# Dividing the score matmuls of the full-attention layers from 64 rows by 128 columns into 64 rows by 32 columns

## The chip, the cores and the metric

The kernel runs on one core of one Trainium2 chip. The metric is the device time of one execution in microseconds (us). Before the change the median of three runs is 2757.61 us (2755.26 to 2764.16).

The engines are named as the profile names them: PE is TensorE's matmul, PEld its weight load, DVE is VectorE, ACT is ScalarE, POOL is GpSimd, SP is SyncE, which issues the DMAs.

## The reference

Four attention layers follow each other on one sequence of 2048 tokens with 512 features: windowed, full, windowed, full. Each is a residual block, with 32 heads of 16 dimensions.

```python
def _B_ref(x, wqkv, wo):                      # the full layer
    qkv = transpose((x @ wqkv).reshape(B, S, 3, H, Dh), 2, 0, 3, 1, 4)
    scores = einsum("bhqd,bhkd->bhqk", q, k) * Dh ** -0.5
    p = softmax(scores, axis=-1)
    o = einsum("bhqk,bhkd->bhqd", p, v)
    return transpose(o, 0, 2, 1, 3).reshape(B, S, D) @ wo
...
x = x + _A_ref(_layernorm(x), A_wqkv, A_wo)   # a window of 256 keys
x = x + _B_ref(_layernorm(x), B_wqkv, B_wo)   # all 2048 keys
x = x + _A_ref(_layernorm(x), A_wqkv, A_wo)
x = x + _B_ref(_layernorm(x), B_wqkv, B_wo)
```

## The kernel before, in words

**A step of a full layer.** `attn_full` (line 750) goes through four chunks of 512 queries, eight groups of four heads, and sixteen tiles of 128 keys: 4 x 8 x 16 = 512 steps in a layer, 1024 in the two full layers (l = 1 and l = 3). A step has these parts:

- Two calls of `exps` (line 706), one for each pair of heads. A head's queries and keys lie in 64 rows: four for each of 16 dimensions, with the high and low halves of float16 and a row for a shift. Two heads fill the 128 partitions. So `exps` issues two matmuls (line 714), one on rows 0 to 63 and one on rows 64 to 127, each with 128 keys as its stationary columns and 512 queries streaming. They write a score tile `ps` of 128 keys by 2 heads by 512 queries, which takes two PSUM banks, a bank for each head.
- One exponential for each `exps` (line 718) on ACT, over 128x1024 values, from `ps` into the SBUF tile `e`.
- Four float32 matmuls (line 758) that multiply `e` with the values: 17 columns (16 dimensions and a column of ones for the denominator) over 128 rows. Head h writes partitions 32h onwards, so that the four lie side by side in column groups of 32. A float32 matmul is two records in the trace, so a step has eight. They accumulate over the sixteen key tiles in `acc[0]`.
- Pieces of side work: the projections and output products of this and the next layer. `mms` (line 419) issues them in full layers as four matmuls of 128 rows by 32 columns (line 429), side by side, into `acc[1]`.

The score matmuls thus use the array as 64 rows by 128 columns, and everything else in a full layer uses it as 128 rows by 32 columns.

**Order.** The order on PE is written out by hand (`manual_schedule`). `attention` (line 955) issues the scores of a step, then the value matmuls of two steps earlier (`flush(2)`), then as much side work as `Side.share` (line 924) allows. `share` pays from a budget by a clock of its own that adds up expected costs (`spent`). The change leaves those costs as they are. The tiles of the other engines are ordered by the framework.

**Buffers.** There are three score tiles: two in the pool `ps_s` and the one called `PH["third"]`; there are six `e` tiles. A score matmul waits until ACT has read the tile three `exps` earlier. After sixteen steps DVE transposes `acc[0]` (line 686), and the first value matmul of the next group of heads waits for that.

**Windowed layers.** `attn_win` uses the same `exps`, there with pieces of 128 to 384 queries, and its projections are 128 rows by 128 columns (line 432).

Of the kernel before, what the change touches and what calls it, by code (L numbers as in the profile page):

```python
# [19 lines left out]
P = 128  # L20
# [9 lines left out]
R = 64  # L30
# [156 lines left out]
def fast_path(ctx, tc, flag, a_x, a_wqkv, a_wo, b_wqkv, b_wo, out):  # L187
# [3 lines left out]
    nc = tc.nc  # L191
# [16 lines left out]
    XC, XN, V, O, OT, KM, PH = {}, {}, {}, {}, {}, {}, {"free": 0.0}  # L208
# [4 lines left out]
    def spent(us):  # L213
        clock[0] += us
        return us
# [490 lines left out]
    def exps(name, kt, qt, pr, pieces):  # L706

        turn["s"] += 1
        ps = PH["third"] if PH["full"] and turn["s"] % 3 == 0 else ps_s.tile([P, 2, QC], F32, name=f"s{name}", tag="s")
        w0 = min(p[3] for p in pieces)  # L710
        w1 = max(p[3] + p[2] for p in pieces)
        for kc, qc, wd_, s0 in pieces:
            for h in range(2):
                nc.tensor.matmul(ps[:, h, s0:s0 + wd_], kt[R * h:R * h + R, pr, kc:kc + P],  # L714
                                 qt[R * h:R * h + R, pr, qc:qc + wd_], start=True, stop=True)
        spent(0.27)
        e = pp.tile([P, 2, QC], F32, name=f"e{name}", tag="e", bufs=EB)
        nc.scalar.activation(e[:, :, w0:w1], ps[:, :, w0:w1], AF.Exp, scale=SCALE)  # L718
        return e
# [30 lines left out]
    def attn_full(l, c, qd, kt, qt, a):  # L750
        for j in range(NT):
            es_ = []
            for pr in range(2):
                es_.append(exps(f"{l}_{c}_{qd}_{j}_{pr}", kt[j // 8], qt, pr, [(j % 8 * P, 0, QC, 0)]))

            def pv(j=j, es_=es_):
                for h in range(4):
                    nc.tensor.matmul(a[32 * h:32 * h + DH + 1, :], V[l, qd // 4, j // 8][:, j % 8, 4 * (qd % 4) + h, :],  # L758
                                     es_[h // 2][:, h % 2, :], start=(j == 0), stop=(j == NT - 1),
                                     skip_group_check=True)  # L760
            yield pv
# [5 lines left out]
    def attn_win(l, c, qd, kt, qt, a):  # L767
        first = True
        for u, tiles in enumerate(WTILES):
            tiles = [p for p in tiles if c or p[0] >= 0]  # L770
            es_ = []
            for pr in range(2):
                e = exps(f"{l}_{c}_{qd}_{u}_{pr}", kt, qt, pr,
                         [(WIN + j * P, q * P, nb * P, s * P) for j, q, nb, s in tiles])
                ev = e.rearrange("p h (m n) -> p h m n", n=P)
                edges = [(s + b, q + b - j == 2) for j, q, nb, s in tiles for b in range(nb) if q + b - j != 1]
                for b, far in edges:
                    v = ev[:, :, b, :]
                    with tc.high_priority(HEAD_START):
                        if far:  # L780
                            nc.gpsimd.affine_select(v, v, pattern=[[0, 2], [-1, P]], compare_op=ALU.is_gt,  # L781
                                                    fill=0.0, base=0, channel_multiplier=1)
                        else:
                            nc.gpsimd.affine_select(v, v, pattern=[[0, 2], [1, P]], compare_op=ALU.is_ge,  # L784
                                                    fill=0.0, base=0, channel_multiplier=-1)
                es_.append(e)

            def pv(u=u, tiles=tiles, es_=es_):
                for x, (j, q, nb, s) in enumerate(tiles):
                    for h in range(4):  # L790
                        nc.tensor.matmul(a[32 * h:32 * h + DH + 1, q * P:(q + nb) * P],  # L791
                                         V[l, (4 * c + j) // 4][:, j % 4, 4 * qd + h, :],
                                         es_[h // 2][:, h % 2, s * P:(s + nb) * P],
                                         start=(u == 0 and x == 0), stop=(u == 2 and x == len(tiles) - 1),
                                         skip_group_check=True)
            yield pv
# [398 lines left out]
```

## Time and profile before

| what | value |
|---|---|
| median of the runs | 2757.61 us |
| span of the profiled execution | 2759.8 us, 0.08% above the median |
| PE, ACT, DVE, POOL busy | 96%, 86%, 35%, 20% of the span |
| score matmuls, all layers (line 714) | 5504, of which 4096 have 512 queries and lie in the full layers |
| exponentials, all layers (line 718) | 2432 |
| value matmul records of the full layers (line 758) | 8192 |
| granted clock of PE in the full layers | 1.00 |

The results list no time of the profiled execution beside its span; the span is used as its own time. The full layers lie from about 507 to 1456 us and from 1792 to 2741 us of the span. Records of PE overlap, since each includes its way through the array: rates are read from starts, or from the length of a merged run of matmuls less one record. "a*b" in a matmul row is rows by columns of the stationary operand.

### The profile page before, as it was taken

To read this page: it belongs to the slowest core of one execution; us is meant where nothing else is said; L and a number is where in the kernel's file an instruction comes from. 1 tells how busy PE (TensorE), PEld (TensorE's weight loads), DVE (VectorE), ACT (ScalarE), POOL (GpSimd) and SP (SyncE) were. 2 spreads that over 40 slices of the span, in tenths; PEclk is the share of its full clock that TensorE was granted. 3 is DMA by queue.
4 is the path that set the end of the run, shared out by engine and by line. 5 is a ranking of instruction groups with operands and counts; after the bars stand their busy time and mean duration, and the time that the engine had idled before them with its cause. 6 is when DMAs were issued, how large, how long until landed. Compare 5 with 4: busy or idle time off the path is not lost.

```text
span 2759.8 us, 59658 instructions
## 1 busy us (share of the span) xinstructions
PE 2636.2 (96%) x24358; PEld 782.5 (28%) x24358; DVE 956.6 (35%) x2059; ACT 2377.0 (86%) x2687; POOL 564.5 (20%) x1129
## 2 busy tenths in 40 slices
PE   8989999999999999999998898999999999999997
PEld 4333344322222222222223333522222222222221
DVE  7678765112131113112215676512222222222122
ACT  3566664799999999999995677399999999999997
POOL 2477672000000000000004677100000000000000
PEclk9999999999999999999999999999999999999999
DMA  6877676322232123212325464613333343333321
GB/s 222 218 251 222 197 229 186 123 71 88 86 102 88 62 82 108 85 60 91 103 67 177 146 190 131 184 62 105 110 112 122 120 123 101 102 110 114 98 95 56
DMA packets 317501, 344.78 MB, mean 125 GB/s; under 512 B 113056, under 2 KB 233376, under 8 KB 311200
## 3 DMA queue, kind: packets, MB, share of 16 engines
q1 hardware_dynamic: 317216, 340.86, 40.4%
q8 instruction: 193, 3.16, 0.5%
q14 instruction: 92, 0.75, 0.1%
HBM read 228.07 MB, written 96.99 MB: 118 GB/s over the span
## 4 chain that ended last, share of the span: by engine, by line
PE 74%; ACT 9%; DVE 6%; issue 5%; POOL 3%; DMA 3%; SPq 0%; ACTq 0%; DVEq 0%; POOLq 0%
PE acc L758 30%; PE s L714 19%; PE acc L429 10%; PE b L432 9%; ACT e L718 8%; PE acc L791 3%; PE bs L432 2%; POOL e L781 1%; DVE ot L686 1%; POOL e L784 1%; POOL wr L344 1%; DVE sp L528 0%; POOL w L346 0%; PE acc L550 0%; DMA kt<-kw 0%
## 5 line engine op out<-in xcount | busy, mean ns | idle before, releaser
L718 ACT ACTIVATE e<-s 128x1024 f32<-128x1024 f32 (+2 forms) x2432 | 2243.5, 1116 | 96.8 <-PE s L714 90.2
L758 PE MATMUL acc<-e,vt 128*17 128x512 f32 x8192 | 1078.0, 598 | 5.3 <-DVE ot L686 4.1
L714 PE MATMUL s<-qt,kt 64*128 64x512 f16 (+3 forms) x5504 | 780.5, 355 | 64.7 <-ACT e L718 41.8
L714 PEld LDWEIGHTS <-kt 64*128 64x128 f16 x5504 | 204.9, 94 | 818.1 <-issue 795.1
L784 POOL TENSOR_SCALAR_AFFINE_SELECT e<-e 128x256 f32<-128x256 f32 x512 | 226.5, 450 | 127.0 <-ACT e L718 126.4
L758 PEld LDWEIGHTS acc<-e,vt 128*17 128x17 f32 x8192 | 136.2, 95 | 379.5 <-issue 347.9
L686 DVE STREAM_TRANSPOSE ot<-acc 128x512 f32<-128x512 f32 x128 | 91.3, 714 | 387.9 <-PE acc L758 317.2
L702 POOL TENSOR_TENSOR oh<-o,oh 128x512 f16<-128x512 f32 x31 | 36.0, 1160 | 886.5 <-DVE oh L701 886.5
L781 POOL TENSOR_SCALAR_AFFINE_SELECT e<-e 128x256 f32<-128x256 f32 x448 | 197.7, 447 | 76.9 <-ACT e L718 74.8
L791 PE MATMUL acc<-e,vt 128*17 128x384 f32 (+2 forms) x2816 | 202.7, 394 | 6.0 <-POOL e L781 4.0
L432 PE MATMUL b<-xc,w 128*128 128x512 f16 x672 | 157.0, 384 | 8.4 <-DVE sp L528 6.9
L533 POOL TENSOR_TENSOR sq_h<-sp_h 128x512 bf16<-128x512 f16 x27 | 28.1, 1039 | 482.7 <-DVE sp_h L527 482.7
L527 DVE TENSOR_SCALAR sp<-acc,es 128x512 f16<-128x512 f32 x28 | 20.9, 748 | 288.5 <-PE acc L429 276.8
L527 DVE TENSOR_SCALAR sp_h<-acc,es 128x512 f16<-128x512 f32 x27 | 20.3, 751 | 286.5 <-PE acc L429 286.5
L525 ACT ACTIVATE sp<-b,es 128x512 f16<-128x512 f32 x56 | 38.5, 687 | 89.6 <-PE b L432 87.4
L429 PE MATMUL acc<-xc,w_h 128*32 128x512 f16 x1296 | 108.6, 379 | 2.3 <-DVE km L566 2.3
L533 POOL TENSOR_TENSOR sq<-sp 128x512 bf16<-128x512 f16 x28 | 29.1, 1039 | 396.5 <-DVE sp L527 396.5
L429 PE MATMUL acc<-xc,w 128*32 128x512 f16 x1344 | 108.9, 379 | 0.3
L638 DVE COPY vt<-acc 128x256 f32<-128x256 f32 (+1 forms) x36 | 18.5, 513 | 257.6 <-PE acc L429 257.6
L673 DVE TENSOR_TENSOR dx<-acc,gcol 128x512 f32<-128x512 f32 x60 | 41.5, 692 | 176.6 <-PE acc L429 176.6
L429 PE MATMUL acc<-wo,oh 128*32 128x512 f16 x1296 | 101.3, 379 | 0.0
L432 PEld LDWEIGHTS <-w 128*128 128x128 f16 x720 | 67.3, 99 | 105.6 <-issue 33.8
(167 smaller groups left out, 1808.2 us busy)
## 6 DMA issues: line engine op xcount, KB each, us to landing
kt<-kf SPq DMA_DIRECT2D x128, 512.0 KB
qt<-qs SPq DMA_DIRECT2D x128, 256.0 KB
xd<-x SPq DMA_DIRECT2D x96, 256.0 KB
x<-xd SPq DMA_DIRECT2D x96, 256.0 KB
w<-wd SPq DMA_DIRECT2D x20, 1024.0 KB
kt<-kw SPq DMA_DIRECT2D x64, 256.0 KB
qs<-sp SPq DMA_DIRECT2D x48, 256.0 KB
wo<-wd SPq DMA_DIRECT2D x12, 1024.0 KB
```

Source lines behind the costliest of these rows:

```text
L429: nc.tensor.matmul(ps[g:g + 32], a[:, g:g + 32], b, start=(i == 0), stop=(i == len(pairs) - 1), skip_group_check=True)
L432: nc.tensor.matmul(ps, a, b, start=(i == 0), stop=(i == len(pairs) - 1))
L527: nc.vector.tensor_scalar(sp[:, 0], ps, e, None, op0=ALU.mult)
L533: nc.gpsimd.tensor_tensor(sq, sp[:, 0], sp[:, 0], ALU.mult)
L673: nc.vector.tensor_tensor(d, ps, gcol[1], ALU.mult)
L686: nc.vector.transpose(ot.rearrange("p b r -> p (b r)"), a)
L714: nc.tensor.matmul(ps[:, h, s0:s0 + wd_], kt[R * h:R * h + R, pr, kc:kc + P], qt[R * h:R * h + R, pr, qc:qc + wd_], start=True, stop=True)
L718: nc.scalar.activation(e[:, :, w0:w1], ps[:, :, w0:w1], AF.Exp, scale=SCALE)
L758: nc.tensor.matmul(a[32 * h:32 * h + DH + 1, :], V[l, qd // 4, j // 8][:, j % 8, 4 * (qd % 4) + h, :], es_[h // 2][:, h % 2, :], start=(j ...
L781: nc.gpsimd.affine_select(v, v, pattern=[[0, 2], [-1, P]], compare_op=ALU.is_gt, fill=0.0, base=0, channel_multiplier=1)
L784: nc.gpsimd.affine_select(v, v, pattern=[[0, 2], [1, P]], compare_op=ALU.is_ge, fill=0.0, base=0, channel_multiplier=-1)
L791: nc.tensor.matmul(a[32 * h:32 * h + DH + 1, q * P:(q + nb) * P], V[l, (4 * c + j) // 4][:, j % 4, 4 * qd + h, :], es_[h // 2][:, h % 2, s ...
```

## The change

In the full layers each score matmul of 64 rows by 128 columns becomes four of 64 rows by 32 columns. Each writes 32 partitions of the same score tile. The loop over the column groups is outside, the two heads inside, so a call of `exps` issues eight matmuls and eight weight loads, where it issued two of each. The windowed layers keep their form.

```diff
         for kc, qc, wd_, s0 in pieces:
-            for h in range(2):
-                nc.tensor.matmul(ps[:, h, s0:s0 + wd_], kt[R * h:R * h + R, pr, kc:kc + P],
-                                 qt[R * h:R * h + R, pr, qc:qc + wd_], start=True, stop=True)
+            for g in range(0, P, 32 if PH["full"] else P):
+                for h in range(2):
+                    out_ = slice(g, g + 32) if PH["full"] else slice(0, P)
+                    nc.tensor.matmul(ps[out_, h, s0:s0 + wd_], kt[R * h:R * h + R, pr, kc + out_.start:kc + out_.stop],
+                                     qt[R * h:R * h + R, pr, qc:qc + wd_], start=True, stop=True,
+                                     skip_group_check=PH["full"])
```

The rest of PE's instructions keep their order, and the wait for a free score tile stays on the first matmul of an `exps`. On ACT and POOL the order is the same too; DVE and SP have a few neighbours exchanged in the first full layer. The changed lines are 713 to 718, and later lines move by three.

## Prediction

> **What bounds the kernel now.** I read the page's busy shares first, then the busy times by stage, then the chain of waits in the two full layers, then the timeline of single steps.
>
> ```profile
> PE 2636.2 (96%) x24358; PEld 782.5 (28%) x24358; DVE 956.6 (35%) x2059; ACT 2377.0 (86%) x2687; POOL 564.5 (20%) x1129
> ```
>
> PE and ACT are both high over the whole span, so only the stages can say which of them decides. The change touches the full layers alone. The next answer has both (about 949 us each, 512 steps each), and three stretches of 100 us out of them; its columns are the stretch, then PE, PEld, DVE, ACT and POOL busy with their counts.
>
> ```profile
> 507.00:1456.00 949.00, 938.90 (x9206) 223.21 (x9208) 184.26 (x426) 943.76 (x1021) 47.48 (x46) 1.00 0.26 83
> 1792.00:2741.00 949.00, 932.72 (x8739) 228.85 (x8740) 220.52 (x435) 941.99 (x1021) 45.44 (x42) 1.00 0.33 103
> ...
> 500.00:600.00 100.00, 98.74 (x1214) 31.52 (x1212) 11.32 (x32) 97.35 (x109) 1.16 (x1) 1.00 0.27 91
> 1100.00:1200.00 100.00, 99.83 (x976) 23.13 (x972) 16.80 (x36) 99.93 (x110) 6.47 (x6) 1.00 0.22 71
> 2600.00:2700.00 100.00, 97.05 (x809) 22.13 (x800) 20.84 (x41) 100.00 (x111) 3.35 (x3) 1.00 0.32 102
> ```
>
> A step takes 949/512 = 1.854 us. ACT, when it has no gap, starts 110 to 111 exponentials in 100 us, 0.901 to 0.909 us each; with 0.905 its two take 1.81 us of the step. So ACT's floor for 1024 steps is 1853 us, where the two layers take 1898. 45 us is the most that a faster PE could bring.
>
> The chain of waits inside each layer, shares by line:
>
> ```profile
> by line: PE acc L758 47.8%; PE s L714 26.9%; PE acc L429 15.7%; ACT e L718 4.6%; issue 1.6%; DVE ot L686 1.1%; DVE sp L527 0.7%; DVE sp L528 0.7%; PE acc L550 0.3%; DVE xh L463 0.1%; DVE st L449 0.1%; DVE dx L652 0.1%; DVE x L653 0.1%; DVE
> by line: PE acc L758 39.9%; PE s L714 23.6%; ACT e L718 13.0%; PE acc L429 12.1%; issue 8.3%; PE acc L550 0.7%; DVE ot L686 0.7%; POOL sq_h L533 0.7%; DVE sp_h L527 0.6%; DVE km L566 0.2%; DVE sp_h L528 0.2%; ACTq L718 0.1%; DVEq L527 0.0%
> ```
>
> PE's own lines carry 47.8 + 26.9 + 15.7 + 0.3 = 90.7% of the first full layer and 39.9 + 23.6 + 12.1 + 0.7 = 76.3% of the second, 83.5% on average. PE is the bound, with ACT close behind: a piece of the chain shows how.
>
> ```profile
> 1210.11 0.98 PE acc L758 x8
> 1211.09 0.43 PE acc L429 x8
> 1211.53 0.54 PE s L714 x4
> 1212.06 0.98 PE acc L758 x8
> 1213.05 0.54 PE s L714 x4
> 1213.59 0.98 PE acc L758 x8
> 1214.57 0.65 PE acc L429 x12
> ```
>
> Scores 0.54 us and values 0.98 make 1.52 without side work, and each group of four side matmuls adds 0.217. A step with no group (1.52) or one (1.74) lies under ACT's 1.81; with two or three (1.95, 2.17) it lies above. Three score tiles even that out in part.
>
> **The change part by part.** What might be saved is a switch between the array's shapes. The timeline of these steps, PE alone, and the rows by shape that give the length of one record:
>
> ```profile
> 1211.99 1.05 PE L758 MATMUL acc<-e,vt 128*17 128x512 f32 x8
> 1212.98 0.61 PE L714 MATMUL s<-qt,kt 64*128 64x512 f16 x4
> 1213.52 1.05 PE L758 MATMUL acc<-e,vt 128*17 128x512 f32 x8
> 1214.39 0.83 PE L429 MATMUL acc<-xc,w 128*32 128x512 f16 x12
> 1215.15 0.61 PE L714 MATMUL s<-qt,kt 64*128 64x512 f16 x4
> ```
>
> ```profile
> L758 PE MATMUL acc<-e,vt 128*17 128x512 f32 x8192 | 1078.0, 598 | 5.3 <-DVE ot L686 4.1
> L714 PE MATMUL s<-qt,kt 64*128 64x512 f16 x4096 | 653.2, 382 | 17.1 <-ACT e L718 1.2 <-ACT vt L636 0.4
> L432 PE MATMUL b<-xc,w 128*128 128x512 f16 x672 | 157.0, 384 | 8.4 <-DVE sp L528 6.9
> ```
>
> ```profile
> L429 PE MATMUL acc<-xc,w_h x1296: 376/379/390, 1789.2 to 2647.7; 128*32 128x512 f16 x186
> ```
>
> *The switches before.* The last score matmul started at 1212.98 + 0.61 - 0.38 = 1213.21 us, and the values 0.31 later, though 512 columns stream in 0.216 (next fence). The last side matmul started at 1214.39 + 0.83 - 0.379 = 1214.84, and the scores again 0.31 later. So each step pays two switches of 0.09 to 0.10 us. From values to side work (128*17 to 128*32) there is none: 0.87 us from 1213.52 to 1214.39 is two passes of 0.43.
>
> *Does a switch remain?* Before, rows and columns both change; after, 64 by 32 stands beside 128 by 32, and only the rows change. The full layers don't show this alone, but the windowed layer does (128*128 to 64*128, first pair of rows), and a change of columns alone too (128*128 to 128*32, second pair):
>
> ```profile
> 406.33 2.76 PE L432 MATMUL b<-xc,w 128*128 128x512 f16 x12
> 409.02 0.55 PE L714 MATMUL s<-qt,kt 64*128 64x384 f16 x6
> ```
>
> ```profile
> 486.76 2.75 PE L432 MATMUL b<-xc,w 128*128 128x512 f16 x12
> 489.45 0.39 PE L550 MATMUL bs<-sq,hsum 128*32 128x512 bf16 x2
> ```
>
> In a run the matmuls are (2.76 - 0.38)/11 = 0.216 us apart. The last one starts at 408.71 and the first of 64 rows at 409.02, 0.31 later: 0.09 for changing the rows alone. For the columns alone it is 489.45 - 489.13 = 0.32, so 0.10. Either change costs as much as both together, hence I take both switches as remaining: nothing saved. The weight loads of a switch don't matter to it, since loads of 128 columns (to the scores) and of 17 (to the values) go with the same 0.31.
>
> The Trainium skill, "TensorEngine Tiling (Array Packing)", Key Properties, says that changing the tiling mode, not merely the tile, drains TensorE, and its list has 64x32 and 128x32 as two configurations. This speaks against the change, and the trace's 0.09 for rows alone agrees; without the rule the sum would be that of the first rival.
>
> *What is added: the stagger.* Eight matmuls side by side stream in the time of one, but each starts a little after the one before. How much, the trace shows for two and for four, behind a switch:
>
> ```profile
> 1788.90 0.39 PE L714 MATMUL s<-qt,kt 64*128 64x512 f16 x2
> 1789.22 0.12 PEld L429 LDWEIGHTS <-w_h 128*32 128x32 f16 x7 [0.23 <-issue]
> 1789.22 0.40 PE L429 MATMUL acc<-xc,w_h 128*32 128x512 f16 x4
> ```
>
> ```profile
> 1204.61 0.62 PE L758 MATMUL acc<-e,vt 128*17 128x512 f32 x4
> ```
>
> Four float16 matmuls last 0.40 us where the longest record of one has 0.390, so 0.010/3 = 3.3 ns apart. The seven loads beside them start within 0.12 - 0.097 = 0.023 us, 3.8 ns apart. Four float32 matmuls last 0.62 against 0.598 to 0.604: 6.7 ns or a little less. I take 3.3 ns, as these are float16. The eighth then starts 7 x 3.3 = 23 ns after the first, where the second started about 3 after. The switch waits for the last, so the scores hold PE for 0.020 us longer in a step. With 6.7 ns it would be 0.044.
>
> The Trainium skill, "TensorE: Matmul & The Clock Gate", Part 3, puts packed matmuls at the time of one plus 4 ns for each further tile: 28 instead of 4 ns here, an estimate of 0.024 us a step, and 20.5 us in the sum below.
>
> *The other additions.* Twelve matmuls and twelve loads a step: the loads run beside matmuls (four took 0.11 us in the timeline, hidden unless a switch exposes the first, as now), and cost nothing while eight run together; the cost without that cover is the second rival's. Their instructions are 24,576 more to fetch:
>
> ```profile
> q8 instruction: 193, 3.16, 0.5%
> q14 instruction: 92, 0.75, 0.1%
> ```
>
> 3.91 MB serve 59,658 instructions, so 1.6 MB more, 0.25% of the DMA engines' time: nothing for the transfers; whether PE gets them in time is the third rival. No wait is added: the first matmul of an exponential's tile waits for ACT as before, and the exponential for the last one. It comes 0.02 us later, which costs ACT only where ACT is already waiting for PE, so it isn't counted twice. DVE's exchanged neighbours and SP's I put at nothing: both have idle time (DVE 185 to 221 of 949 us busy).
>
> *The sum.* 512 x 0.020 x 0.907 = 9.3 us and 512 x 0.020 x 0.763 = 7.8 us: **17 us**. On the profiled 2759.8 that is 2777; the median of the runs is 2 us lower, which gives **2774**. Where ACT carries the chain the 0.02 is hidden by its backlog; without that cover it would be 20.5 us. With 6.7 ns it is 0.044 x 1024 x 0.835 = 38 us. At the lower end the switches could be up to 0.02 shorter, by the spread of 0.09 to 0.10 on each, and the sum would be zero. The forecast's own range is thus 2757 to 2798.
>
> **The rivals.**
>
> *The switches go (not slower).* If array and loads care only for the width in columns, 0.19 of a step vanishes and 0.02 is added. PE's step would be 1.52 - 0.17 = 1.35 plus on average 0.29 (15.7% of 1.854) or 0.22 (12.1%) of side work, well under ACT's 1.81, so ACT decides. At 110 exponentials in 100 us, 2048 take 1862 us: 36 less than 1898, **2722**. It decides as soon as one switch goes, for one alone takes most steps under 1.81. Against it stands the 0.09 for rows alone; for it, that no row shows 64 by 32.
>
> *The eight don't run together.* Two row groups run at once (the score pair) and four column groups (side work), but no row shows both. If the row groups took turns, each `exps` would stream twice: 0.43 a step more, on average (1.52 + 0.29 + 0.43) and (1.52 + 0.22 + 0.43), 512 x (2.24 + 2.17) = 2258 us instead of 1898: **3118**. It needs a limit that neither part shows.
>
> *Instructions come too slowly.* A step has (9206 + 9208)/512 = 36 records on PE in the first layer and 34 in the second; 24 more make 60 and 58. At 1.85 us that is one in 31 ns. The densest 100 us above show 2426 records, 41 ns each, and PE was fed then. If 41 were the limit, 512 x 0.041 x (60 + 58) = 2477 us, 579 more; 31 is free; half way is about +290, **3047**. For it: the rate was never needed. Against it: in the run of four above, matmuls and loads start 3 to 4 ns apart.
>
> *It does nothing measurable.* The stagger is hidden by shorter switches or by ACT's backlog: within 8 us, **2757**. This is the lower end of the forecast.
>
> **How the numbers follow.** About 0.3%, 8 us, is what a measurement of this kernel can tell from no change. Switches stay and the stagger costs over 8 us: 0.55. The same, under 8 us: 0.14. Switches go: 0.13. Row groups in turns: 0.07. Instructions too slow: 0.11. Faster 0.13, same 0.14, slower 0.55 + 0.07 + 0.11 = 0.73. The range must leave out no more than 2 in 10: the two dear rivals (0.18) are left out above, and it reaches down to the switches going, 2722, so 2720 to 2800.
>
> **What would show it.** In the changed profile, a run of sixteen score matmuls should still have its values 0.31 us after its last start, and side work to scores 0.31: then the switches remain. If these are 0.22, they went, and ACT should show 110 or 111 exponentials in each 100 us, with waits for ACT on PE. The run of eight should spread over 0.02 us (3.3 ns) or 0.05 (6.7). If the second eight start 0.43 after the first, the row groups take turns. If PE has idle time put down to "issue" ahead of matmuls, instructions come too slowly. What would make the forecast wrong above all is the one thing taken from other shapes: the price of a switch into and out of 64 by 32.

## The result and the profile after

The changed kernel takes 2772.57 us (median of five runs, 2770.47 to 2778.56) against 2757.65 before (five runs, 2755.26 to 2764.16). The ratio is 1.0054, with a 95% interval of 1.0040 to 1.0068: 15 us slower, where 17 us, 2774, was forecast. The profiled execution grew from 2759.8 to 2770.8 us.

The page after, parts 1, 3 and 5: twelve matmuls a step more, and the shape of each.

```profile
span 2770.8 us, 84237 instructions
...
PE 2653.3 (96%) x36646; PEld 803.5 (29%) x36646; DVE 956.7 (35%) x2059; ACT 2385.7 (86%) x2687; POOL 567.1 (20%) x1129
...
q8 instruction: 289, 4.73, 0.7%
...
L716 PE MATMUL s<-qt,kt 64*32 64x512 f16 (+3 forms) x17792 | 799.5, 374 | 60.1 <-ACT e L721 41.7
```

PE is busy 17 us longer, PEld, which runs beside it, 21 us, ACT 9; DVE and POOL hardly changed. The next answer has the two full layers and two stretches of 100 us in the first and second of them (PE, PEld, DVE, ACT, POOL busy).

```profile
504.00:1463.00 959.00, 950.16 (x15328) 235.36 (x15327) 184.59 (x426) 950.01 (x1021) 47.62 (x46) 1.00 0.27 83
1799.00:2752.00 953.00, 940.17 (x14853) 238.53 (x14854) 220.60 (x435) 944.55 (x1022) 45.60 (x42) 1.00 0.34 103
...
1100.00:1200.00 100.00, 99.86 (x1616) 24.20 (x1612) 18.28 (x41) 99.84 (x109) 6.50 (x6) 1.00 0.22 68
2600.00:2700.00 100.00, 97.79 (x1466) 23.15 (x1458) 24.81 (x50) 100.00 (x111) 4.35 (x4) 1.00 0.35 110
```

The windows are set at the layers' new places: the first layer ends later by about 9 us of its own, the second by about 4. In 1100 to 1200 us ACT now starts 109 exponentials where it started 110, with PE at 99.86; both engines are nearly full there, and which of them sets the pace is read from the chain below. At 2600 ACT still has its 111: the longer PE is hidden.

The chain of waits inside the two layers:

```profile
by line: PE acc L761 47.7%; PE s L716 27.8%; PE acc L429 15.5%; ACT e L721 4.6%; issue 1.1%; DVE ot L686 1.0%; DVE sp L527 0.6%; DVE sp L528 0.6%; PE acc L550 0.3%; DVE xh L463 0.1%; DVE st L449 0.1%; DVE dx L652 0.1%; DVE x L653 0.1%; DVE 
by line: PE acc L761 40.9%; PE s L716 24.4%; PE acc L429 12.0%; ACT e L721 11.2%; issue 8.6%; PE acc L550 0.7%; DVE ot L686 0.7%; POOL sq_h L533 0.7%; DVE sp_h L527 0.6%; DVE km L566 0.2%; DVE sp_h L528 0.1%; ACTq L721 0.0%; DVEq L527 0.0%
```

PE's lines now have 91.3% and 78.0%. The scores rose in both layers, from 26.9 to 27.8% and from 23.6 to 24.4%; in the second the values rose too (39.9 to 40.9%), at the cost of ACT (13.0 to 11.2%). Single steps on PE, and then the first eight score matmuls of one of them:

```profile
1204.34 0.40 PE L429 MATMUL acc<-wv,xc 128*32 128x512 f16 x4
1204.67 0.62 PE L716 MATMUL s<-qt,kt 64*32 64x512 f16 x16
1205.22 1.05 PE L761 MATMUL acc<-e,vt 128*17 128x512 f32 x8
1206.09 0.61 PE L429 MATMUL acc<-wv,xc 128*32 128x512 f16 x8
1206.64 0.62 PE L716 MATMUL s<-qt,kt 64*32 64x512 f16 x16
1207.19 0.62 PE L761 MATMUL acc<-e,vt 128*17 128x512 f32 x4
```

```profile
1204.67 0.41 PE L716 MATMUL s<-qt,kt 64*32 64x512 f16 x8
```

From the first score to the first value it is 0.55 us (0.54 before). Eight matmuls last 0.41 us together where one record has 0.387, so their starts spread over 0.023 us, 3.3 ns each, and sixteen last 0.62, so the second eight begin about 0.22 after the first: all eight run at once. The last score starts at 1204.67 + 0.62 - 0.376 = 1204.91, and the values 0.31 later; side work to scores is 1206.09 + 0.61 - 0.379 = 1206.32 to 1206.64, 0.32. Both switches stayed.

Two digits don't separate a few ns, so the table below takes the starts of all steps from the traces, in whole ns (medians over about 510 steps in each layer, for "from side" over the 300 to 360 that have such side work; both layers gave the same to 1 ns). "Spread" is from the first to the last score start of a step, "to values" from there to the first value matmul, "from side" from the last side matmul of 512 columns to the first score. Each ratio is against runs of the kernel before that were taken with that kernel's; the three rows from "heads outside" to "256 queries" share theirs.

| kernel | score matmuls of one exponential | spread | to values | from side | ratio to before, 95% interval |
|---|---|---|---|---|---|
| before | 2 of 64*128 | 230 | 306 | 312 | 1 |
| changed | 8 of 64*32 | 249 | 306 | 309 | 1.0054 (1.0040 to 1.0068) |
| heads outside | 8 of 64*32 | 249 | 306 | 309 | 1.0044 (1.0031 to 1.0057) |
| 64 columns | 4 of 64*64 | 250 | 306 | 309 | 1.0042 (1.0029 to 1.0055) |
| 256 queries | 16 of 64*32 | 361 | 199 | 309 | 1.0083 (1.0069 to 1.0097) |
| one bank, base | 1 of 64*128 | 227 | 306 | 312 | 0.9992 (0.9981 to 1.0002) |
| one bank, 32 columns | 4 of 64*32 | 236 | 306 | 309 | 1.0020 (1.0011 to 1.0029) |
| one bank, 64 columns | 2 of 64*64 | 243 | 306 | 309 | 1.0037 (1.0026 to 1.0048) |
| one bank, 128 rows | 4 of 128*32 | (waits) | 205 | 192 | 0.9920 (0.9907 to 0.9934) |

### The profile page after: what moved, and what is told of

Same layout as the page of the kernel before. It is cut to its first block, busy times and chain, and to the rows that moved or that the text cites. A ratio compares the mean times of both kernels' runs of the same rounds, so it can differ in the third digit from the quotient of the medians.

```text
span 2770.8 us, 84237 instructions
## 1 busy us (share of the span) xinstructions
PE 2653.3 (96%) x36646; PEld 803.5 (29%) x36646; DVE 956.7 (35%) x2059; ACT 2385.7 (86%) x2687; POOL 567.1 (20%) x1129
## 3 DMA queue, kind: packets, MB, share of 16 engines
q8 instruction: 289, 4.73, 0.7%
## 4 chain that ended last, share of the span: by engine, by line
PE 75%; ACT 8%; DVE 5%; issue 5%; POOL 3%; DMA 3%; SPq 0%; ACTq 0%; DVEq 0%; POOLq 0%
PE acc L761 31%; PE s L716 20%; PE acc L429 10%; PE b L432 9%; ACT e L721 8%; PE acc L794 3%; PE bs L432 2%; POOL e L784 1%; POOL e L787 1%; DVE ot L686 1%; POOL wr L344 1%; DVE sp L528 0%; DVE xh L469 0%; POOL w L346 0%; DMA xd<-x 0%
## 5 line engine op out<-in xcount | busy, mean ns | idle before, releaser
L716 PE MATMUL s<-qt,kt 64*32 64x512 f16 (+3 forms) x17792 | 799.5, 374 | 60.1 <-ACT e L721 41.7
L716 PEld LDWEIGHTS <-kt 64*32 64x32 f16 (+1 forms) x17792 | 226.3, 89 | 809.4 <-issue 786.1
```

Of the source, the lines that this page charges most:

```text
L716: nc.tensor.matmul(ps[out_, h, s0:s0 + wd_], kt[R * h:R * h + R, pr, kc + out_.start:kc + out_.stop], qt[R * h:R * h + R, pr, qc:qc + wd_] ...
```

## The experiments

The theory: a step's scores hold PE from their first to their last start, and then a switch of fixed length follows; dividing them only moves the last start. Rivals: a price for each added instruction, a price for dividing columns at all, a switch that depends on the column width. Diffs are against the changed kernel.

**Two column groups instead of four.**

```diff
-            for g in range(0, P, 32 if PH["full"] else P):
+            for g in range(0, P, 64 if PH["full"] else P):
...
-                    out_ = slice(g, g + 32) if PH["full"] else slice(0, P)
+                    out_ = slice(g, g + 64) if PH["full"] else slice(0, P)
```

> Each score matmul is divided into two of 64 rows by 64 columns, so an exponential's tile has four matmuls (two before, eight in the changed kernel). Theory of the stagger: starts 3.3 ns apart, so the last of four starts 10 ns after the first, 7 ns more than before the change; the changed kernel's 20 ns cost 15 us, so this costs 5 us: ratio to before 1.002, and values still 0.31 us after the last score start. Rival, that dividing the columns at all has a fixed price (a longer switch, exposed loads): about 1.005, as the changed kernel. Rival, that the column width sets the price of the switch, so that 64 columns beside 32 cost more than 32 beside 32: above 1.005.

Measured: 1.0042, not 1.002. The expectation missed: with half the matmuls it cost nearly as much. The timeline of PE in two steps, and the rows by shape:

```profile
1205.05 0.63 PE L716 MATMUL s<-qt,kt 64*64 64x512 f16 x8
1205.61 0.62 PE L761 MATMUL acc<-e,vt 128*17 128x512 f32 x4
```

```profile
L716 PE MATMUL s<-qt,kt 64*64 64x512 f16 x8192 | 672.4, 390 | 12.5 <-ACT e L721 1.2 <-ACT vt L636 0.8
...
L716 PEld LDWEIGHTS <-kt 64*64 64x64 f16 x8192 | 180.4, 104 | 651.8 <-issue 646.5 <-DMA kt<-kf 0.7 <-DMA out_dram<-x 0.6
...
L716 PEld LDWEIGHTS <-kt 64*128 64x128 f16 x1408 | 53.9, 94 | 150.0 <-issue 136.2 <-DMA kt<-kw 4.0 <-DMA wv<-wd 0.6
```

The four starts are 3.3 ns apart as expected, but the second four begin 240 ns after the first, where it is 227 with 32 or with 128 columns. A load of 64 columns has a record of 104 ns, one of 128 columns 94 in the same kernel. The first load behind a switch has no matmul beside it to hide under: the record of the first score matmul is 400 ns long here, and 387 with 32 or 128 columns. So the spread comes to 250 in another way: 10 from the starts and 13 from the load. This run could not tell a fixed price of dividing columns from the two terms; the runs with one bank did.

**The order of the loops.**

```diff
-            for g in range(0, P, 32 if PH["full"] else P):
-                for h in range(2):
+            for h in range(2):
+                for g in range(0, P, 32 if PH["full"] else P):
```

> The same sixteen matmuls of 64 rows by 32 columns a step as in the changed kernel, with the loop over the two heads outside and the one over the four column groups inside. Theory of the stagger: each start follows the one before by 3.3 ns whichever of row or column group changes, so the same 23 ns and the same ratio as the changed kernel, 1.005. Rival, that the order decides (neighbours in one row group start 6.7 ns apart, as the float32 value matmuls do): 47 ns from first to last, about 0.024 us a step more, ratio 1.011 to 1.012.

Measured: 1.0044, its interval lying over the changed kernel's, and the same 249, 306 and 309 ns. Neighbours in one row group start 3.3 ns apart too: the order doesn't matter.

**The queries in halves.**

```diff
+            for b in range(0, wd_, wd_ // 2 if PH["full"] else wd_):
...
+                        n_ = wd_ // 2 if PH["full"] else wd_
-                    nc.tensor.matmul(ps[out_, h, s0:s0 + wd_], ...
-                                     qt[R * h:R * h + R, pr, qc:qc + wd_], ...
+                        nc.tensor.matmul(ps[out_, h, s0 + b:s0 + b + n_], ...
+                                         qt[R * h:R * h + R, pr, qc + b:qc + b + n_], ...
```

> The changed kernel with each of its score matmuls divided once more into two of 256 queries: 32 score matmuls a step, twice the changed kernel's, and 92 records a step on PE instead of 60. Theory of the stagger: the last of a group of eight still starts 23 ns after its first, and two pieces of 256 stream in 2 x 0.109 us instead of 0.216, so 2 to 3 ns more for each exponential, 5 ns a step, some 4 us over the changed kernel: ratio to before 1.007. Rival, that each added matmul and load has its price (12 of each cost 15 us in the changed kernel, 16 more cost 20): 1.0125. Rival, that PE gets its instructions at a limited rate (a record in 31 ns was enough in the changed kernel, this one needs one in 20 ns): at 25 ns a step would take 2.3 us, ratio above 1.15, and PE idle with nothing to wait for.

Measured: 1.0083; 1.0125 lies outside the interval, 1.007 just inside. From first score to first value it is 361 + 199 = 560 ns against 249 + 306 = 555 in the changed kernel: 5 more, as expected. But 5 ns a step make 4 us, and against the kernel with the heads outside, which has the changed kernel's sixteen matmuls and was compared with the same runs of before, the halves cost 1.0083 less 1.0044, or 11 us. One stretch in the first full layer, the score rows of this kernel, and PE in one step:

```profile
1100.00:1200.00 100.00, 99.75 (x2448) 34.88 (x2440) 17.58 (x40) 99.60 (x108) 6.48 (x6) 1.00 0.24 73
```

```profile
L718 PE MATMUL s<-qt,kt 64*32 64x256 f16 x32768 | 678.1, 272 | 16.0 <-issue 4.0 <-ACT e L723 1.2 <-DMA kt<-kf 0.7
```

```profile
2237.73 0.61 PE L718 MATMUL s<-qt,kt 64*32 64x256 f16 x27
2239.72 0.29 PE L718 MATMUL s<-qt,kt 64*32 64x256 f16 x5 [1.37 <-issue]
2239.94 1.05 PE L763 MATMUL acc<-e,vt 128*17 128x512 f32 x8
```

PE takes 4888 records in 100 us, one in 20 ns, and is 99.75% busy. But the 4.0 us put down to "issue" are eight breaks in the middle of runs of scores, like the one shown, where PE waits for no other engine. These eight steps are together 5.7 us longer than the same steps with the heads outside. In the trace each break ends 2.2 to 2.5 us after a transfer of 16 KB on the instruction queue has begun, so instructions that came late are the likely cause. Another 2.0 us are a longer wait for DVE, of the kind that "The costs put at nothing" below describes. So the third rival is true here in a small part. The changed kernel, with 3228 records in this stretch or 31 ns each, has no such break, nor has any other kernel of the table.

**One bank, 128 rows or 64.** These two and the two after them write one bank of the score tile and read it twice, so that PE's scores can take another shape while ACT, the values and the side work keep their sizes. They leave out separate scores for the two heads of a pair, so they serve for times alone.

```diff
-                for h in range(2):
+                for h in range(1 if PH["full"] else 2):
...
+                    r_ = slice(0, P) if PH["full"] else slice(R * h, R * h + R)   # slice(0, R) in the control
-                    nc.tensor.matmul(ps[out_, h, s0:s0 + wd_], kt[R * h:R * h + R, pr, kc + out_.start:kc + out_.stop],
+                    nc.tensor.matmul(ps[out_, h, s0:s0 + wd_], kt[r_, pr, kc + out_.start:kc + out_.stop],
...
-        nc.scalar.activation(e[:, :, w0:w1], ps[:, :, w0:w1], AF.Exp, scale=SCALE)
+        src = ps[:, 0:1, w0:w1].broadcast_to([P, 2, w1 - w0]) if PH["full"] else ps[:, :, w0:w1]
+        nc.scalar.activation(e[:, :, w0:w1], src, AF.Exp, scale=SCALE)
```

> Part of the computation is changed: in the full layers the scores of a pair of heads are one set of four matmuls of 128 rows by 32 columns (the two heads' products summed), written to one bank of the score tile, and the exponential reads this bank twice, so that ACT, the values and the side work keep their sizes. The scores' streaming time is that of before (512 columns), but their shape is now that of everything else in the layer. Theory: the two switches of a step (0.09 to 0.10 us each) are gone, values start about 0.22 us after the last score matmul, PE is under ACT, and ACT decides: 2722 to 2735 us, ratio 0.987 to 0.992. Rival, that the 0.09 belongs to the change of operands or banks and not of shape: the switches stay, ratio 1.00.

> The control to the run with 128 rows, with the same part of the computation changed (one bank of the score tile written and read twice by the exponential), but the four score matmuls have 64 rows by 32 columns (the first head alone). It differs from that run in the rows alone. Theory: the change of rows alone keeps both switches at 0.09 to 0.10 us, four starts spread over 10 ns where before the change it was 3, so ratio to before 1.000 to 1.003, values 0.31 us after the last score start. Rival, that 32 columns beside 32 need no switch: as the run with 128 rows, ratio 0.987 to 0.992.

Measured: 0.9920 with 128 rows, at the edge of what was expected, and 1.0020 with 64. The two differ in rows alone. PE's timeline of each, 128 rows first:

```profile
1203.50 0.62 PE L429 MATMUL acc<-wv,xc 128*32 128x512 f16 x8
1203.93 0.73 PE L717 MATMUL s<-qt,kt 128*32 128x512 f16 x8
...
1206.10 0.40 PE L717 MATMUL s<-qt,kt 128*32 128x512 f16 x4 [0.36 <-ACT e L723]
1206.31 1.04 PE L763 MATMUL acc<-e,vt 128*17 128x512 f32 x8
```

```profile
1204.61 0.61 PE L429 MATMUL acc<-wv,xc 128*32 128x512 f16 x8
1205.15 0.61 PE L717 MATMUL s<-qt,kt 64*32 64x512 f16 x8
1205.69 1.05 PE L763 MATMUL acc<-e,vt 128*17 128x512 f32 x8
```

With 128 rows the scores start 0.19 us after the last side matmul (1203.50 + 0.62 - 0.38 = 1203.74), and the values 0.21 after a run of scores began: it all streams through. With 64 rows the scores start 0.31 after the last side matmul (1204.84 to 1205.15). So 64 by 32 beside 128 by 32 pays the full switch, though the columns are alike. The chain of waits in the two layers of the kernel with 128 rows:

```profile
by line: ACT e L723 44.4%; issue 41.7%; PE acc L763 5.9%; PE s L717 4.5%; PE acc L429 2.7%; DVE sp L527 0.2%; DVE sp L528 0.2%; PE acc L550 0.2%; ACTq L723 0.0%; DVEq L527 0.0%
by line: ACT e L723 44.6%; issue 32.9%; PE acc L763 9.3%; PE s L717 7.3%; PE acc L429 4.1%; POOL sq_h L533 0.7%; DVE sp_h L527 0.5%; PE acc L550 0.3%; DVE km L566 0.2%; ACTq L723 0.1%
```

Without switches PE falls from 91% of the chain (changed kernel) to 13% in the first layer and from 78% to 21% in the second. ACT has taken over; in the first layer it has hardly a gap left:

```profile
506.00:1443.00 937.00, 882.90 (x11248) 336.60 (x11244) 183.46 (x426) 935.63 (x1021) 48.00 (x46) 1.00 0.27 84
```

**One bank: the base, and 64 columns.** The control with `slice(g, g + P)` in one step, and with `slice(g, g + 64)` in steps of 64.

> Part of the computation is left out as in the run with 64 rows and one bank (the first head's scores serve both heads, the exponential reads one bank twice), but the scores of a pair are one matmul of 64 rows by 128 columns: the base for the runs with one bank. Theory: no stagger at all, the second exponential's matmul starts 0.227 us after the first one's, switches as before, so 3 ns less a step than before the change: ratio 0.998 to 1.001. Rival, that reading one bank twice changes ACT's pace: the number of exponentials started in 100 us without a gap is no longer 110 to 111, and the ratio is off by over 0.005.

> As the one-bank base, with the one score matmul divided into two of 64 rows by 64 columns. Question: the run with 64 columns cost 1.0042 where the stagger alone gave 1.002, and its second group of four started 0.240 us after the first instead of 0.226, with weight load records of 103 to 106 ns instead of 88 to 96. Theory: loads of 64 columns take longer than those of 128 or 32, and the first one after a switch is not hidden, 13 ns once a step; with two starts 3 ns apart the scores take 16 ns more than in the base, 0.016 x 1024 x 0.835 = 14 us: ratio to the base 1.004 to 1.005. Rival, that four starts side by side were needed for the delay: 1.001.

Measured: the base has 0.9992 (0.9981 to 1.0002), so reading one bank twice changes nothing that the time can tell. Its ACT in a stretch without a gap:

```profile
2600.00:2700.00 100.00, 96.40 (x687) 17.31 (x685) 20.78 (x41) 100.00 (x111) 3.35 (x3) 1.00 0.30 97
```

111 exponentials, as before. Against this base, four column groups of 32 cost 1.0020/0.9992 = 1.0028, two of 64 cost 1.0037/0.9992 = 1.0045. The intervals of the two overlap a little; in the profiles the two full layers take 6.0 and 10.2 us more than the base's 1895.4. A fixed price of dividing columns would be the same in both, and the smaller number of pieces costs more: it is the spread that counts, 9 ns over the base in the one and 16 in the other. The page's rows for loads of the two, 64 columns first:

```profile
L717 PEld LDWEIGHTS <-kt 64*64 64x64 f16 x4096 | 173.6, 104 | 654.7 <-issue 648.7 <-DMA kt<-kf 0.8 <-DMA qs<-sp_h 0.6
```

```profile
L717 PEld LDWEIGHTS <-kt 64*32 64x32 f16 x8192 | 152.3, 90 | 666.1 <-issue 658.5 <-DMA qs<-sp_h 0.6 <-DMA out_dram<-x 0.6
```

The 14 ns between the load records agree with the 13 ns that the second group begins later, and with the first score matmul's record, 400 against 387 ns. The cost of the 64-column run is therefore accounted for, with one pair of matmuls as with two: the miss of the first expectation was a term left out, not the theory. That the load is the cause is read from these records; no run changed the load alone.

## Why the prediction was right, point by point

**PE bound, ACT close behind.** Shown from both sides: the 16 ns that the table adds to a step's path on PE (19 more in the spread, 3 less from side work to scores) made the kernel slower, and with the switches gone ACT took the chain over.

**The switches remain.** The step that decided the sign. It was taken from 128*128 to 64*128 in a windowed layer, and held for 64 by 32: 306 ns to the values before and after, 309 instead of 312 from side work. The control with 64 rows and the run with 128 show it as a matter of shape, rows alone sufficing.

**The stagger.** 3.3 ns a start and 20 ns a step were forecast; the spread grew from 230 to 249 ns, and 6.7 ns a start is out.

**The sum.** 17.1 us forecast, 14.9 measured (1.0054 of 2757.65; 11 to 19 by the interval). The number is right in part by luck: the stagger was taken too high, and a cost put at nothing made up for some of it. By layers, in the one profiled execution of each kernel, from first to last value matmul: 949.4 to 958.5 us in the first, 9.0 against 9.3 forecast, and 949.1 to 952.9 in the second, 3.8 against 7.8. The profiles with the heads outside and with 64 columns have 9.2 and 3.8, and 8.1 and 3.7. Followed step by step, the first layer falls behind by 0.4 to 0.5 us in most groups of 32 steps, up to 16 ns a step, 7.2 us in all; a single jump of 1.8 us comes with a longer wait for DVE (next point). The second layer falls behind at that pace up to its middle, 3.4 us, and by only 0.4 us in its second half, where PE has 924 side matmuls instead of 1656 and ACT runs without a gap (2600 to 2700 us above). So in the profiles the stagger cost 11 us, not 17, and both together 12.8, inside the interval. A step costs 16 ns and not 20, because a switch into 64 by 32 comes 3 ns sooner; and PE's share of the chain, 76% in the second layer, was too high a weight there: with 16 ns it gives 6.3 us, where 3.8 were lost.

**The costs put at nothing.** Instruction transfers grew from 3.16 to 4.73 MB on their queue, the 1.6 MB foreseen, and no idle time of PE ahead of a matmul is put down to "issue" in the changed kernel. Loads beside matmuls stayed hidden, but for the first one behind a switch, and this one costs more than before only if it is 64 columns wide. DVE's exchanged neighbours were not free, though. DVE's last operations before a transposition of `acc[0]` (line 686), and the value matmuls that wait for it, before and then after:

```profile
1336.56 0.98 DVE L463 TENSOR_SCALAR xh<-x,mv,y 128x512 f16<-128x512 f32 x2
1337.46 0.70 DVE L686 STREAM_TRANSPOSE ot<-acc 128x512 f32<-128x512 f32 x1
1338.22 1.05 PE L758 MATMUL acc<-e,vt 128*17 128x512 f32 x8 [1.49 <-DVE ot L686]
```

```profile
1340.21 0.98 DVE L463 TENSOR_SCALAR xh<-x,mv,y 128x512 f16<-128x512 f32 x2
1341.12 0.68 DVE L469 TENSOR_TENSOR xh<-xn,xh 128x512 f16<-128x512 f32 x1
1341.72 0.70 DVE L686 STREAM_TRANSPOSE ot<-acc 128x512 f32<-128x512 f32 x1
1342.48 1.91 PE L761 MATMUL acc<-e,vt 128*17 128x512 f32 x8 [2.09 <-DVE ot L686]
```

```profile
1342.00:1344.00 2.00, 1.52 (x8) 0.15 (x8) 2.00 (x5) 0.68 (x1) 0.00 (x0) 0.52 1.10 202
1344.00:1346.00 2.00, 2.00 (x28) 0.30 (x24) 2.00 (x7) 0.92 (x2) 0.00 (x0) 0.63 0.96 242
```

The transposition now stands behind one more operation of 0.68 us, and PE waits 0.6 us longer (2.09 against 1.49). Then PE's granted clock is down to 0.52 and 0.63 in the next two stretches of 2 us (before the change it stays at 1.00 there), and the same eight value matmuls take 1.91 us. The kernel with the heads outside shows both too; the one with 64 columns has the longer wait but keeps its clock at 1.00, and its first layer grew by 8.1 us instead of 9.0. So a microsecond or two of what the change cost is not the stagger's.

**The rivals.** Switches go: refuted, and its price was too high. It was 36 us with ACT at its best pace throughout; the run with 128 rows gained 0.9920 of 2758.9, 22 us, for its two layers take 937 and 939 us where 1862 for both was assumed: ACT's exponentials start 0.903 us apart there in the median, but some 50 in a layer start later, 11 to 13 us together. Row groups in turns: refuted by 227 ns between the groups of eight. Instructions too slow: refuted for the changed kernel's one record in 31 ns; at one in 20 ns eight breaks cost 5.7 us. Nothing measurable: the interval, 1.0040 to 1.0068, excludes it.

## What to carry to other kernels

Look in the trace for a switch of the same kind, rows alone or columns alone, before dividing matmuls to match their neighbours: here both dimensions had to be alike for the 0.1 us to go, and one alike was worth nothing. Pieces that run side by side take the time of one plus a start each, and this is added where the next switch waits for the last of them. When PE and another engine are within a few per cent, a cost on PE shows in full where PE leads and not at all where the other does, while a saving ends at the other engine: 16 ns more a step cost 11 us, and some 200 ns less brought only 22. To know where PE leads, follow the two kernels step by step; its share of the chain of waits gave too much. And a change on one engine can exchange the order of work on another: look there for a wait that grew.

## What the runs showed of the hardware that was not expected

Among the scores' weight loads, all of 64 rows, one of 64 columns takes longer than one of 128 or of 32: records of 104 ns against 94 and 89 to 90, and 13 ns more behind a switch. The Trainium skill, "TensorE: Matmul & The Clock Gate", Weight-path perf modes, says that the fast weight load is on when there are 128 weights that are not FP32, and reads four chunks of 32 columns side by side; 64 columns would then go without it. The runs agree in the order. By the section on LDWEIGHTS of the same page of the Trainium skill, a time of columns over 1.2, 64 columns would take 27 ns more than 32, an estimate; here it was 14.

PE took one record in 20 ns over 100 us, at 99.75% busy, but at this pace it broke off eight times in the two layers, for 0.2 to 1.4 us each, likely for want of instructions. Pieces of 256 queries cost a step 5 ns more than pieces of 512. After a pause of 2.5 us between the starts of matmuls (1.9 before the change) PE's granted clock fell to about a half for a few microseconds in two of the three profiles that have this pause; what decides it was not followed up.
